# A chunked linear recurrence: inverting 32x32 triangular blocks on VectorE, or 16x16 blocks there and the rest as small products on TensorE

## The chip, the cores and the metric

The kernel runs on one core of a Trainium2 chip. The metric is the device time of one execution in microseconds; the time of a kernel is the median of its runs, and smaller is better.

## The reference

A recurrence over 768 steps for 4 batches of 8 heads, with a 40x40 state each, and behind it a mixture of eight experts over the 3072 tokens that it makes. All of it is float32.

```python
for t in range(S):                       # S = 768, B = 4, H = 8, D = 40
    y[:, :, t] = einsum('bhd,bhde->bhe', r[t], state)
    Sa = einsum('bhde,bhe->bhd', state, a[t])
    state = state * w[t][:, :, None, :] - einsum('bhd,bhe->bhde', Sa, b[t])
    state = state + einsum('bhd,bhe->bhde', v[t], k[t])
...
x = y.transpose(0, 2, 1, 3).reshape(B * S, H * D)      # 3072 x 320
P = np.exp(x @ w_gate - max)
for _ in range(8):                       # rows, then columns, normalised
    P /= P.sum(1, keepdims=True) + 1e-09
    P /= P.sum(0, keepdims=True) + 1e-09
    P *= N / E
for e in range(E):                       # E = 8, F = 1024
    out += P[:, e:e + 1] * (np.maximum(x @ w1[e], 0.0) @ w2[e])
```

## The kernel before

**Two parts.** The recurrence comes first (the function `attention`), and then the experts (`body`). The expert part is two large products per expert (L571 and L636), each made of three products of high and low parts, with ScalarE and VectorE between them. The change does not touch it. Its weights (L499) and its tokens (`xs`, L534 and L536, read back from the DRAM tensor `xd` into which the recurrence writes y) are loaded on SyncE's queue, SP, and the first of these loads stand among the recurrence's last ones.

**Chunks.** The recurrence is cut into 12 chunks of 64 steps. Within a chunk the state update is a system of 64 equations with a unit triangular matrix I - L for each batch and head, so a chunk needs T, the 64x64 inverse, for 4 x 8 = 32 pairs of batch and head. Two heads lie side by side on the 128 partitions, so a batch has 4 pairs of heads (NP = 4), and a T tile `tt` holds, for each of 16 pairs, a 128x128 matrix that is block diagonal: two heads, each with two 32x32 blocks on its diagonal and one 32x32 block beside them.

**The step of one batch in one chunk** (`recur`, 48 in all) is a chain: `av` (L280, products with the state) is masked by VectorE into `f`; `xc` (L288) makes the right-hand sides, which ScalarE copies to `x1` and `c1` (L294, L295); `pu` (L299) multiplies by T; VectorE masks it to `pm` (L301); `c2` (L306), `ws` on VectorE (L308), `y` and `z` on GpSimd, `zt` (L326, a transpose), and two copies by ScalarE into `rv` (L329, the state for this batch's next chunk). `lp` (L336) is the gate's product for the experts. The four batches run staggered.

**Preparations** (`prep`, one for each chunk and batch, ahead of the steps) load `inp`, make two scans on VectorE (`q`, `g`), scaled copies `kb` and `ab` (GpSimd, the first ones partly VectorE), the products `ll` (L158) and the transposes `kt` (L166), and from these by ScalarE and VectorE the operands `sx`, `bb`, and `lt` (L172), which goes to the DRAM tensor `ld`: that is L, for the inverse. From the seventh on ScalarE issues that store (L177).

**The inverse.** The chunks are taken two at a time (GROUPS). A group has 128 diagonal blocks of 32x32, and they are put on the 128 partitions, one each: `load_lu` loads them from `ld` into `lu`. VectorE inverts all of them at once: `inv_diag` column by column inside 8x8 blocks, `inv_8` joins these to 16x16 and `inv_16` (three calls with two contractions each) joins those to 32x32. A contraction (`contract`) is a broadcast multiplication and a reduction over its last axis (L192, L195). `un` is the inverse and `tn` its transpose, as far as each is needed, and `finish` stores both to DRAM (`ud`, `nd`; L362, L363).

**The rest of T.** For each chunk `tload` loads the diagonal 32x32 blocks into `tt` (L246, four loads) and what the block beside them needs into `lt` (L, L239 on; the transposed first block, L241) and `t2` (L242, the second block). `tmat` then makes that block by two products on 32x32 tiles of TensorE, 32 matmuls each: `gp` (L255), copied to `mt` by ScalarE (L257), and `op` (L261), copied into `tt` by ScalarE with four copies (L264). One such small matmul uses 32 rows and 32 columns of TensorE; up to four of them lie on different tiles of it.

**What sets the order.** `attention` writes the events (steps, loads, products, preparations, pieces of the inverse) into a list `ev` with a time each, five to a chunk, sorts it and issues them in that order; `tmat` does its work at a raised priority (T_PRI). The framework's scheduler then gives each engine a fixed order of instructions from that, which the engine keeps. Two `tt` buffers, 19 sets of preparation buffers and a pool of two PSUM buffers (`pt`: `gp`, `op`, `lp` and the first `kt`) bound what can run ahead. In the chunk loop SP's queue holds the loads of T and of the steps, and the stores of `un` and `tn`, in one order as well.

Of the kernel before, what the change touches and what calls it, by code (L numbers as in the profile page):

```python
# [11 lines left out]
F32 = mybir.dt.float32  # L12
# [17 lines left out]
def attention(ctx, tc, d, xd, ps, pq, pt, gs, lg):  # L30
    nc = tc.nc
# [10 lines left out]
    mask_f = cst[0:R2, 64:128]
    mask_p = cst[:, 128:232]
    ident = cst[:, 232:360]
    one65 = cst[0:RL, 400:660]

# [3 lines left out]
    for n in range(NCH * NB - NSX, NCH * NB):  # L50
        i, pool = n % NSX, sets[n - NCH * NB + NSX]
# [12 lines left out]
    tt_b = [const.tile([128, 4 * NP, 128], F32, name=f"tt{i}") for i in range(NTB)]  # L64
    ltt = const.tile([128, 2, 4 * NP, 32], F32, name="lt2")
    lt_b = [[ltt[i * 64:i * 64 + 64, k] for k in range(2)] for i in range(2)]
    t2_b = [const.tile([128, 2 * NP, 32], F32, name=f"t2{i}") for i in range(2)]
    mt = const.tile([128, 2 * NP, 32], F32, name="mt")
    ab_b = [pin.tile([R2, NP, 128], F32, name=f"ab{i}") for i in range(2)]
# [31 lines left out]
    def first_use(i):  # L101
        if i in fresh:
            fresh.discard(i)
            nc.gpsimd.memset(bb_b[i], 0.0)
            nc.scalar.copy(out=sx_b[i][64:R2].rearrange("r p h x -> r (p h) x")[:, :, 64:104],
                           in_=cst[64:R2, 360:400].unsqueeze(1).broadcast_to([40, 8, 40]))

    state = {"sx": 0, "ab": 0, "g1": 0, "rv": 0, "c1": 0, "lt": 0, "t2": 0, "tt": 0, "y": 0}

    def rot(key, lst):  # L110
        i = state[key]
        state[key] = (i + 1) % len(lst)
        return lst[i]
# [133 lines left out]

    def tmat(c):
        tt, (lb, t1, t2) = tts[c], tls[c]
        hq = [slice(q * 32, q * 32 + 32) for q in range(4)]  # L250
        with tc.high_priority(T_PRI):
            gp = pt.tile([128, 2 * NP, 32], F32, name="gp", tag="pt")
            for g in range(4 * NP):
                for h in range(2):
                    nc.tensor.matmul(gp[hq[g % 2 * 2 + h], g // 2], lhsT=lb[hq[h], g], rhs=t1[hq[h], g],  # L255
                                     start=True, stop=True)
            nc.scalar.copy(out=mt, in_=gp)  # L257
            op = pt.tile([128, 2 * NP, 32], F32, name="op", tag="pt")
            for g in range(2 * NP):
                for q in range(4):  # L260
                    nc.tensor.matmul(op[hq[q], g], lhsT=mt[hq[q], g], rhs=t2[hq[q], g], start=True, stop=True)  # L261
            for q in range(4):
                r = q % 2 * 64
                nc.scalar.copy(out=tt[r:r + 32, q // 2::2, r + 32:r + 64], in_=op[hq[q]])  # L264

# [93 lines left out]
    def finish(s, us):  # L359
        nc.vector.tensor_copy(out=tn[us, 16:32, 0:16], in_=un[us, 0:16, 16:32].rearrange("u c j -> u j c"))  # L360
        for o in range(0, us.stop, 64):
            nc.sync.dma_start(out=invs[s][1][o:o + 64], in_=un[o:o + 64])  # L362
# [29 lines left out]
    for s, cs in enumerate(GROUPS):  # L392
        us = slice(0, 64 * len(cs))
        t0 = 5 * cs[0] - 10
        n = len(cs) * NB
        for i in range(n):
            cb = (cs[0] + i // NB, i % NB)
            j = cb[0] * NB + cb[1] - NSX
            t = 5 * (j // 4) + 3 + SKEW * (j % 4) + 0.01
            t = max(t, t0 + P0[s] + PD * i) if s else -20 + 0.01 * i  # L400
            ev.append((t, do_prep, (s,) + cb + (i == 0,)))
        t += 0.02
        ev.append((t, load_lu, (s, len(cs))))
# [14 lines left out]
INV_DT = 0.05  # L418
# [35 lines left out]
def body(ctx, tc, d, out):  # L454
# [303 lines left out]
def _layout(inputs):  # L758
# [40 lines left out]
    cst[64:128, 64:128] = 1.0
    cst[0:64, 128:192] = up  # L800
    cst[64:128, 128:192] = up
    cst[:, 192:232] = 1.0
    cst[:, 232:360] = np.eye(128)
    cst[64:104, 360:400] = np.eye(40)
    cst[:, 400::65] = 1.0
    arrays = dict(inp=inp, rv=np.concatenate([rb, packed(g["v"])], -1), vt=vt, wts=wts, gate=gate, cst=cst)
# [18 lines left out]
```

## Time and profile before

| | |
|---|---|
| median of 3 runs | 1821.08 us (1817.26 to 1829.43) |
| the profiled execution | 1816.42 us, span 1814.0 us |
| mean granted clock of TensorE | 0.954 |
| busy in the span: TensorE matmuls | 1686.0 us, 93% |
| VectorE | 1366.1 us, 75% |
| ScalarE | 842.8 us, 46% |
| GpSimd | 876.6 us, 48% |
| DMA | 135.61 MB in 178736 packets, 119189 of them under 512 bytes |
| chain that ended last | 72% TensorE: L636 37%, L571 34% |
| first expert product (L571) | at 477.6 us |

The granted clock is the share of its full speed at which TensorE was allowed to run. Busy shares are means over two parts with different limits, and the profile has to be read by stretches. In the profile's rows an arrow points from what is read to what is written (`pu<-x,tt`), a number behind an x counts instructions, and what stands behind a second arrow is what ended the idle time before them. Numbers of buffers are left out there (`lt2` is `lt`, `t20` is `t`, `x1` is `x`).

### The profile page before, as it was taken

What the parts mean: (1) busy time and instruction counts of PE and PEld (TensorE: products, weight loads), DVE (VectorE), ACT (ScalarE), POOL (GpSimd) and SP (SyncE); (2) the same over time, 40 slices, a digit from 0 to 9 for tenths busy, and PEclk for the clock granted to TensorE, in tenths of its full rate; (3) what the DMA queues carried; (4) which work ended last, traced back from release to release, by engine and by line L of the source; (5) the groups of instructions that cost most, each with busy time, mean ns of one, the idle gap of its engine ahead of it and who ended that gap; (6) DMA issues with size and microseconds to landing.
All of it is one profiled execution on the core that took longest, in us unless ns stands there. A gap on an engine that the chain in (4) does not pass through costs nothing.

```text
span 1814.0 us, 32745 instructions
## 1 busy us (share of the span) xinstructions
PE 1686.0 (93%) x12611; PEld 1662.1 (92%) x12611; DVE 1366.1 (75%) x2353; ACT 842.8 (46%) x1811; POOL 876.6 (48%) x850
## 2 busy tenths in 40 slices
PE   5478888987889999999999999999999999999999
PEld 4367888887889999999999999999999999999999
DVE  7886976974788777767686778867686777768675
ACT  6357767765634443424343443435343443434342
POOL 7555645724453554728173554009173553719160
PEclk7569989998989999999999999999999999999999
DMA  7478678668221111102010112202010111102001
GB/s 200 106 160 197 150 173 192 153 142 200 75 67 36 41 38 38 58 20 76 8 69 20 57 38 72 58 1 76 14 63 22 55 38 38 58 20 76 18 21 44
DMA packets 178736, 135.61 MB, mean 75 GB/s; under 512 B 119189, under 2 KB 160789, under 8 KB 178581
## 3 DMA queue, kind: packets, MB, share of 16 engines
q1 hardware_dynamic: 174901, 127.79, 26.8%
q10 hardware_dynamic: 3680, 5.74, 1.2%
q8 instruction: 99, 1.62, 0.4%
q14 instruction: 56, 0.46, 0.1%
HBM read 111.48 MB, written 22.02 MB: 74 GB/s over the span
## 4 chain that ended last, share of the span: by engine, by line
PE 72%; DVE 6%; DMA 2%; issue 1%; SPq 1%; ACT 1%; POOL 1%; DVEq 0%; ACTq 0%; POOLq 0%
PE op L636 37%; PE p L571 34%; DVE pr L192 1%; DVE sm L589 1%; DVE hl L595 1%; DVE gt L195 0%; DMA ld<-lt 0%; PE xc L288 0%; DMA rv<-in_rv_dram 0%; DVE un L195 0%; PE pu L299 0%; DVE u L589 0%; DMA ws<-in_wts_dram 0%; DVE xch L559 0%; DMA lu<-ld 0%
## 5 line engine op out<-in xcount | busy, mean ns | idle before, releaser
L571 PE MATMUL p<-xch,wh 128*128 128x384 f32 (+1 forms) x1792 | 605.7, 339 | 10.2 <-DVE u L589 4.3
L592 ACT ACTIVATE hh<-sm 128x384 fp32r<-128x384 f32 x512 | 269.4, 527 | 723.0 <-DVE sm L589 722.9
L636 PE MATMUL op<-wh,hh 128*128 128x320 f32 x1536 | 477.1, 311 | 1.1 <-ACT hh L592 0.9
L636 PE MATMUL op<-wl,hh 128*128 128x320 f32 x1536 | 474.8, 310 | 0.0
L636 PE MATMUL op<-wh,hl 128*128 128x320 f32 x1536 | 468.2, 310 | 0.9 <-DVE hl L595 0.9
L517 POOL TENSOR_TENSOR wl<-ws,wh 128x640 fp32r<-128x640 f32 x60 | 103.6, 1726 | 606.3 <-ACT wh L515 606.1
L595 DVE SCALAR_TENSOR_TENSOR hl<-sm,hh 128x384 fp32r<-128x384 f32 x512 | 375.0, 766 | 1.8 <-ACT hh L592 1.3
L571 PEld LDWEIGHTS p<-xch,wh 128*128 128x128 f32 (+1 forms) x1792 | 337.2, 188 | 14.3 <-DVE u L589 6.0
L571 PE MATMUL p<-xcl,wh 128*128 128x384 f32 x896 | 302.6, 338 | 0.0
L571 PE MATMUL p<-xch,wl 128*128 128x384 f32 x896 | 301.7, 337 | 0.0
L636 PEld LDWEIGHTS op<-wh,hh 128*128 128x128 f32 x1536 | 290.3, 189 | 2.2 <-ACT hh L592 1.9
L636 PEld LDWEIGHTS op<-wl,hh 128*128 128x128 f32 x1536 | 291.1, 190 | 0.0
L636 PEld LDWEIGHTS op<-wh,hl 128*128 128x128 f32 x1536 | 287.3, 188 | 1.3 <-DVE hl L595 1.2
L589 DVE TENSOR_TENSOR sm<-p,u 128x384 f32<-128x384 f32 x384 | 236.1, 625 | 8.8
L571 PEld LDWEIGHTS p<-xcl,wh 128*128 128x128 f32 x896 | 168.7, 188 | 0.0
L571 PEld LDWEIGHTS p<-xch,wl 128*128 128x128 f32 x896 | 168.6, 188 | 0.0
L589 DVE TENSOR_TENSOR sm<-p,p 128x384 f32<-128x384 f32 x128 | 71.3, 557 | 128.7 <-PE p L571 74.7
L589 DVE TENSOR_TENSOR p<-p,p 128x384 f32<-128x384 f32 x128 | 71.2, 556 | 99.6 <-PE p L571 99.1
L589 DVE TENSOR_TENSOR u<-p,p 128x384 f32<-128x384 f32 x128 | 70.8, 554 | 57.6 <-PE p L571 56.4
L158 PE MATMUL ll<-ab,kb 104*128 104x128 f32 x336 | 62.4, 343 | 51.8 <-POOL ab L153 32.3
L158 PEld LDWEIGHTS ll<-ab,kb 104*128 104x128 f32 x336 | 53.4, 241 | 58.3 <-POOL ab L153 35.8
L525 POOL TENSOR_TENSOR wl<-ss,wh 128x512 fp32r<-128x512 f32 x60 | 90.1, 1502 | 27.6 <-ACT wh L522 23.4
(164 smaller groups left out, 2637.0 us busy)
## 6 DMA issues: line engine op xcount, KB each, us to landing
ws<-in_wts_dram SPq DMA_DIRECT2D x60, 832.0 KB, 4.4
inp<-in_inp_dram SPq DMA_DIRECT2D x42, 451.5 KB, 4.8
rv<-in_rv_dram SPq DMA_DIRECT2D x48, 336.0 KB, 4.1
xd<-y SPq DMA_DIRECT2D x24, 224.0 KB, 3.1
ld<-lt ACTq DMA_DIRECT2D x40, 128.0 KB, 2.9
f<-in_vt_dram SPq DMA_DIRECT2D x48, 80.0 KB, 3.1
out_dram<-acc SPq DMA_DIRECT2D x42, 80.0 KB, 2.1
lu<-ld SPq DMA_DIRECT2D x24, 128.0 KB, 3.2
```

Source lines behind the costliest of these rows:

```text
L158: nc.tensor.matmul(ll[:, p], lhsT=kb[:, p], rhs=ab[:, p], start=True, stop=True)
L192: nc.vector.tensor_tensor(out=prv, in0=a.unsqueeze(2).broadcast_to([nu, n_c, n_r, n_k]), in1=m.unsqueeze(1).broadcast_to([nu, n_c, n_r, n_ ...
L517: g.tensor_tensor(out=wl[:, 0:640], in0=raw[:, 256:896], in1=wh[:, 0:640], op=ALU.subtract)
L525: g.tensor_tensor(out=lv[:, 3:7], in0=so[:, :, 0], in1=hv[:, 3:7, 0], op=ALU.subtract)
L571: nc.tensor.matmul(o, lhsT=w_, rhs=x_, start=(j == 0), stop=(j == 3))
L589: eng.tensor_tensor(out=out, in0=x, in1=y, op=ALU.add)
L592: nc.scalar.activation(out=hh[:, f, h], in_=sm[f][:, h], func=AF.Relu)
L595: v.scalar_tensor_tensor(out=hl[:, f, h], in0=sm[f][:, h], scalar=0.0, in1=hh[:, f, h], op0=ALU.max, op1=ALU.subtract)
L636: nc.tensor.matmul(ops[i], lhsT=a[:, h, cs], rhs=w_[:, cw], start=(f == 0 and h == 0 and j == 0), stop=(last and h == 1 and j == 2))
```

## The change

`N_FINE = 6` covers all six groups, so that every group takes the new way:

- **VectorE** stops at 16x16: the three `inv_16` no longer run. In their place `flip_8` has GpSimd copy the 16x16 block of L beside the two inverted ones into the free corner of `un`, and `side` copies the second inverted block into the free corner of `tn` (`finish` made a copy of that size before). `flip_8` also has the first copy of the former `flip_l`; the second one (L200) goes.
- **TensorE** makes the 32x32 inverses out of these: `ga` and `wb`, 64 products of 16x16 each on four tiles, give the corner of each 32x32 block and put it into `tt`. `tp` transposes the first 32x32 block of each head, by 32 products with the identity. `gp` and `op`, 32 products each, make the block beside the diagonal as before, but lie on two tiles each.
- **ScalarE** copies each result out of PSUM by tile: four copies behind `ga`, four behind `wb`, two each behind `tp`, `gp` and `op`, in place of one and four.
- **Loads of T** are 7 a chunk, not 8: two of L (`lm`), one of `nd` for all 64 blocks (`vt`), four of the diagonal blocks (`tt`), the last in this order. `load_lu` puts the two blocks of a head on neighbouring partitions.
- The constants lose 64 columns: two masks share their storage. The function `flat` and the old way stay in the code, for groups from N_FINE on, and do not run.

In the new numbering `ga`, `wb`, `gp` and `op` are all L267, `tp` is L283, `ll` L156, `kt` L164, `pu` L329, `xc` L318, `av` L310, `c2` L336, `zt` L356 and `lp` L366; the loads are L249 (`lm`), L251 (`vt`), L254 (`tt`), and the copies L275, L279, L286, L290 and L294.

```diff
+    def flip_8(us):
+        lh = half_t(luf, us)
+        nc.vector.tensor_copy(out=lh[:, :, 8:16, 0:8], in_=lh[:, :, 0:8, 8:16].rearrange("u b k r -> u b r k"))
+        nc.gpsimd.tensor_copy(out=un[us, 0:16, 16:32], in_=lu[us, 0:16, 16:32])
+    def side(us):
+        nc.vector.tensor_copy(out=tn[us, 0:16, 16:32], in_=un[us, 16:32, 16:32])
-    INV = [(flip_l, ())] + [(inv_diag, (i,)) for i in range(1, 8)] + [(flip_d, ())]
-    INV += [(inv_8, (0,)), (inv_8, (1,)), (flip_h, ()), (inv_16, (0,)), (inv_16, (1,)), (inv_16, (2,))]
+    INV8 = [(inv_diag, (i,)) for i in range(1, 8)] + [(flip_d, ()), (inv_8, (0,)), (inv_8, (1,)), (flip_h, ())]
+    INV16 = [(flip_8, ())] + INV8 + [(side, ())]
...
     def tload(c):
...
-        u = [slice(cc * 64 + blk * 32, cc * 64 + blk * 32 + 32) for blk in range(2)]
-        for h in range(2):
-            nc.sync.dma_start(out=lb[h * 32:h * 32 + 32],
+        u = slice(cc * 64, cc * 64 + 64)
+        for h in range(0, 2):
+            nc.sync.dma_start(out=lm[h * 64:h * 64 + 32],
                               in_=ld[cc, 0:32].rearrange("j b p h s -> j (b p) h s")[:, :, h, 32:64])
-        nc.sync.dma_start(out=t1, in_=nd[u[0]].rearrange("(g h) j s -> (h j) g s", h=2))
-        nc.sync.dma_start(out=t2, in_=ud[u[1]].rearrange("(g q) j s -> (q j) g s", q=4))
-        for h in range(2):
-            for blk in range(2):
-                r = slice(h * 64 + blk * 32, h * 64 + blk * 32 + 32)
-                nc.sync.dma_start(out=tt[r, :, r], in_=ud[u[blk]].rearrange("(g h) j s -> (h j) g s", h=2)[h * 32:h * 32 + 32])
+        nc.sync.dma_start(out=vt, in_=nd[u].rearrange("(g q) j s -> (q j) g s", q=4))
+        for q in range(4):
+            r = slice(q * 32, q * 32 + 32)
+            nc.sync.dma_start(out=tt[r, :, r], in_=ud[u].rearrange("(g q) j s -> q j g s", q=4)[q])
...
+        hq = [slice(q * 32, q * 32 + 32) for q in range(4)]
+        xq = [slice(q * 32, q * 32 + 16) for q in range(4)]
+        yq = [slice(q * 32 + 16, q * 32 + 32) for q in range(4)]
+        lo, hi = slice(0, 16), slice(16, 32)
+        def products(name, tiles, lhs, rhs, n):
+            o = pt.tile([128, 4 * NP, n], F32, name=name, tag="pt")
+            for g in range(4 * NP):
+                for r, q in tiles:
+                    nc.tensor.matmul(o[r, g], lhsT=lhs(q, g), rhs=rhs(q, g), start=True, stop=True)
+            return o
         with tc.high_priority(T_PRI):
...
+                ga = products("ga", [(xq[q], q) for q in range(4)],
+                              lambda q, g: tt[xq[q], g, yq[q]], lambda q, g: vt[xq[q], g, lo], 16)
                 for q in range(4):
+                    nc.scalar.copy(out=vt[xq[q], :, lo], in_=ga[xq[q]])
+                wb = products("wb", [(xq[q], q) for q in range(4)],
+                              lambda q, g: vt[xq[q], g, lo], lambda q, g: vt[xq[q], g, hi], 16)
+                for q in range(4):
+                    nc.scalar.copy(out=tt[xq[q], :, yq[q]], in_=wb[xq[q]])
+                tp = pt.tile([128, 4 * NP, 32], F32, name="tp", tag="pt")
+                for g in range(4 * NP):
+                    for q in (0, 2):
+                        nc.tensor.matmul(tp[hq[q], g], lhsT=tt[hq[q], g, hq[q]], rhs=ident[hq[q], hq[q]],
+                                         start=True, stop=True)
+                for q in (0, 2):
+                    nc.scalar.copy(out=vt[hq[q]], in_=tp[hq[q]])
+            gp = products("gp", [(hq[q + 1], q) for q in (0, 2)],
+                          lambda q, g: lm[hq[q], g], lambda q, g: vt[hq[q], g], 32)
+            for q in (1, 3):
+                nc.scalar.copy(out=lm[hq[q]], in_=gp[hq[q]])
+            op = products("op", [(hq[q - 1], q) for q in (1, 3)],
+                          lambda q, g: lm[hq[q], g], lambda q, g: tt[hq[q], g, hq[q]], 32)
+            for q in (0, 2):
+                nc.scalar.copy(out=tt[hq[q], :, hq[q + 1]], in_=op[hq[q]])
...
-                u0, r0 = cc * 64 + blk * 32, blk * 32
-                nc.sync.dma_start(out=lu[u0:u0 + 32],
+                r0 = blk * 32
+                nc.sync.dma_start(out=lu[cc * 64 + blk:cc * 64 + 64:2],
...
+N_FINE = 6
```

**Where the products stand.** TensorE's order at the start, with the preparations (`ll`, `kt`) and the first T. Before, the first `gp` stands behind the 17th `ll`, and `op` and the first `pu` behind the 18th:

```order
L158 MATMUL ll_972<-ab0_204,kb_962 128x128 x4
L166 MATMUL kt_977<-cst_144,kb_962 128x104 x4
L255 MATMUL gp_850<-lt2_200 32x32 x32
L158 MATMUL ll_1029<-ab1_205,kb_1019 128x128 x4
L166 MATMUL kt_1034<-cst_144,kb_1019 128x104 x4
L261 MATMUL op_884<-t20_201,mt_203 32x32 x32
L255 MATMUL gp_1208<-lt2_200 32x32 x32
L299 MATMUL pu_946<-x1_931,tt0_198 128x104
```

Now, at the same place, from the first `ga`, which stands behind the 15th `ll`:

```order
L267 MATMUL ga_825<-vt0_202,tt0_198 16x16 x64
L156 MATMUL ll_757<-ab1_205,kb_747 128x128 x4
L164 MATMUL kt_762<-cst_144,kb_747 128x104 x4
L267 MATMUL wb_894<-vt0_202 16x16 x64
L156 MATMUL ll_1119<-ab0_204,kb_1109 128x128 x4
L164 MATMUL kt_1124<-cst_144,kb_1109 128x104 x4
L283 MATMUL tp_963<-cst_144,tt0_198 32x32 x32
L156 MATMUL ll_1176<-ab1_205,kb_1166 128x128 x4
L164 MATMUL kt_1181<-cst_144,kb_1166 128x104 x4
L267 MATMUL gp_998<-vt0_202,lm0_200 32x32 x32
L156 MATMUL ll_1250<-ab0_204,kb_1240 128x128 x4
L164 MATMUL kt_1255<-cst_144,kb_1240 128x104 x4
```

`op` is the next row, behind the 19th `ll`; between two of T's five products there is one preparation.

TensorE's order in the chunk loop, at chunk 2's T. Before, its two products stand within one step of a batch, and the second one breaks a product `xc` in two:

```order
L306 MATMUL c2_1779<-pm_1659,bb6_186 104x104 x3
L255 MATMUL gp_1701<-lt2_200 32x32 x32
L158 MATMUL ll_1638<-ab0_204,kb_1630 128x128 x4
L166 MATMUL kt_1643<-cst_144,kb_1630 128x104 x4
L306 MATMUL c2_1779<-pm_1659,bb6_186 104x104
L299 MATMUL pu_1819<-x1_1677,tt1_199 128x104 x4
L288 MATMUL xc0_1826<-f_1691,sx8_193 104x104
L261 MATMUL op_1735<-t20_201,mt_203 32x32 x32
```

Now, from `ga` to just behind `wb`:

```order
L267 MATMUL ga_2006<-vt0_202,tt0_198 16x16 x64
L156 MATMUL ll_1739<-ab0_204,kb_1731 128x128 x4
L164 MATMUL kt_1744<-cst_144,kb_1731 128x104 x4
L356 MATMUL zt_1794<-cst_144,z_1723 40x104 x4
L336 MATMUL c2_1801<-pm_1760,bb4_178 104x104 x4
L329 MATMUL pu_1849<-x1_1778,tt1_199 128x104 x4
L267 MATMUL wb_2075<-vt0_202 16x16 x64
L318 MATMUL xc0_1862<-f_1784,sx6_185 104x104 x4
```

`tp`, `gp` and `op` follow at distances like this, so the five products spread over about three steps of a batch. The last use of this buffer `tt0` for an earlier chunk stands about two steps ahead of `ga`, and the first `pu` with the new T one step behind `op`.

SP's queue where the last T is loaded and the expert part's first loads (`ws`, `xs`) begin. Before:

```order
L241 DMA lt2_200<-nd_3375 64x16x32
L242 DMA t21_202<-ud_3374 128x8x32
L269 DMA rv4_211<-in_rv_dram 112x4x192
L269 DMA rv0_207<-in_rv_dram 112x4x192
L499 DMA ws_5552<-in_wts_dram 128x1664
L246 DMA tt1_199<-ud_3374 32x16x32 x4
L499 DMA ws_5568<-in_wts_dram 128x1664
```

Now:

```order
L569 DMA xs_7564<-xd_57 128x2x256
L571 DMA xs_7564<-xd_57 32x2x256 x4
L345 DMA xd_57<-y0_214 448x1x128
L569 DMA xs_7582<-xd_57 128x2x256
L571 DMA xs_7582<-xd_57 32x2x256 x3
L301 DMA f_6395<-in_vt_dram 64x8x40
L571 DMA xs_7582<-xd_57 32x2x256
L249 DMA lm1_201<-ld_4339 32x16x32
L299 DMA rv1_208<-in_rv_dram 112x4x192
L249 DMA lm1_201<-ld_4339 32x16x32
L251 DMA vt1_203<-nd_4341 128x16x32
L254 DMA tt0_198<-ud_4340 32x16x32 x4
```

The first two `ws` and these two `xs` now stand ahead of the last diagonal blocks' loads; before, the first `ws` stood ahead of the last one, and the first `xs` behind it.

More of the change, by code (lines that the diff above doesn't have):

```diff
@@ L37, in attention @@
     dr = ctx.enter_context(tc.tile_pool(name="a_dr", bufs=2, space=bass.MemoryType.DRAM))
-    cst = const.tile([128, 64 + 64 + 104 + 128 + 40 + 260], F32, name="cst")
+    cst = const.tile([128, 64 + 104 + 128 + 40 + 260], F32, name="cst")
     nc.sync.dma_start(out=cst, in_=d["cst"])
     mask_u = cst[0:64, 0:64]
[L42 to L45, printed above, removed]
+    mask_f = cst[0:R2, 0:64]
+    mask_p = cst[:, 64:168]
+    ident = cst[:, 168:296]
+    one65 = cst[0:RL, 336:596]
     NTB = 2
@@ L64, in attention @@
     tt_b = [const.tile([128, 4 * NP, 128], F32, name=f"tt{i}") for i in range(NTB)]
[L65 to L68, printed above, removed]
+    lm_b = [const.tile([128, 4 * NP, 32], F32, name=f"lm{i}") for i in range(2)]
+    vt_b = [const.tile([128, 4 * NP, 32], F32, name=f"vt{i}") for i in range(2)]
     ab_b = [pin.tile([R2, NP, 128], F32, name=f"ab{i}") for i in range(2)]
@@ L105, in first_use @@
             nc.scalar.copy(out=sx_b[i][64:R2].rearrange("r p h x -> r (p h) x")[:, :, 64:104],
-                           in_=cst[64:R2, 360:400].unsqueeze(1).broadcast_to([40, 8, 40]))
-    state = {"sx": 0, "ab": 0, "g1": 0, "rv": 0, "c1": 0, "lt": 0, "t2": 0, "tt": 0, "y": 0}
+                           in_=cst[64:R2, 296:336].unsqueeze(1).broadcast_to([40, 8, 40]))
+    state = {"sx": 0, "ab": 0, "g1": 0, "rv": 0, "c1": 0, "lm": 0, "vt": 0, "tt": 0, "y": 0}
     def rot(key, lst):
@@ L232, in tload, with flat @@
+    def side(us):
+        nc.vector.tensor_copy(out=tn[us, 0:16, 16:32], in_=un[us, 16:32, 16:32])
+    def flat(us):
+        nc.gpsimd.memset(tn[us, 0:16, 16:32], 0.0)
+    INV8 = [(inv_diag, (i,)) for i in range(1, 8)] + [(flip_d, ()), (inv_8, (0,)), (inv_8, (1,)), (flip_h, ())]
+    INV16 = [(flip_8, ())] + INV8 + [(side, ())]
+    INV = [(flip_l, ())] + INV8 + [(inv_16, (0,)), (inv_16, (1,)), (inv_16, (2,))]
     def tload(c):
-        tt, (lb, t1), t2 = rot("tt", tt_b), rot("lt", lt_b), rot("t2", t2_b)
@@ L248, in tmat @@
+        for q in range(4):
+            r = slice(q * 32, q * 32 + 32)
+            nc.sync.dma_start(out=tt[r, :, r], in_=ud[u].rearrange("(g q) j s -> q j g s", q=4)[q])
     def tmat(c):
-        tt, (lb, t1, t2) = tts[c], tls[c]
+        tt, (lm, vt) = tts[c], tls[c]
         hq = [slice(q * 32, q * 32 + 32) for q in range(4)]
-        with tc.high_priority(T_PRI):
[L252 to L259, printed above, removed]
-                for q in range(4):
[L261 to L264, printed above, removed]
+        xq = [slice(q * 32, q * 32 + 16) for q in range(4)]
@@ L359, in finish @@
     def finish(s, us):
-        nc.vector.tensor_copy(out=tn[us, 16:32, 0:16], in_=un[us, 0:16, 16:32].rearrange("u c j -> u j c"))
+        if s >= N_FINE:
+            nc.vector.tensor_copy(out=tn[us, 16:32, 0:16], in_=un[us, 0:16, 16:32].rearrange("u c j -> u j c"))
         for o in range(0, us.stop, 64):
@@ L403, in attention @@
         ev.append((t, load_lu, (s, len(cs))))
-        for i, (fn, a) in enumerate(INV):
-            ev.append((t + INV_DT * 10 * i / len(INV), fn, (us,) + a))
+        if s == N_FINE:
+            ev.append((t, flat, (us,)))
+        ops = INV16 if s < N_FINE else INV
+        for i, (fn, a) in enumerate(ops):
+            ev.append((t + INV_DT * 10 * i / len(ops), fn, (us,) + a))
         ev.append((t + INV_DT * 10 + 0.01, finish, (s, us)))
@@ L478, in body @@
     nc.gpsimd.memset(ones, 1.0)
-    nc.sync.dma_start(out=ident, in_=d["cst"][:, 232:360])
+    nc.sync.dma_start(out=ident, in_=d["cst"][:, 168:296])
     po = ctx.enter_context(tc.tile_pool(name="po", bufs=1, space=bass.MemoryType.PSUM))
@@ L793, in _layout @@
     gate[0:40], gate[64:104] = wg[0], wg[1]
-    cst = np.zeros((128, 660), np.float32)
+    cst = np.zeros((128, 596), np.float32)
     i = np.arange(64)
@@ L797, in _layout @@
     cst[0:64, 0:64] = up
+    cst[64:128, 0:64] = 1.0
     cst[0:64, 64:128] = up
[L799 to L805, printed above, removed]
+    cst[64:128, 64:128] = up
+    cst[:, 128:168] = 1.0
+    cst[:, 168:296] = np.eye(128)
+    cst[64:104, 296:336] = np.eye(40)
+    cst[:, 336::65] = 1.0
     arrays = dict(inp=inp, rv=np.concatenate([rb, packed(g["v"])], -1), vt=vt, wts=wts, gate=gate, cst=cst)
```

4 lines of the change are left out of this document (3 added, 1 removed).

## The prediction

> **What bounds the kernel now.** I read the slices of the page first, to see where the recurrence ends.
>
> ```profile
> PE   5478888987889999999999999999999999999999
> PEclk7569989998989999999999999999999999999999
> DMA  7478678668221111102010112202010111102001
> ```
>
> A slice is 45 us. From the twelfth on TensorE is full at full clock: that is the expert part, which the change does not touch. So the time can only move in the first 485 us: at the start (TensorE half idle), along the chunks (eight to nine tenths, clock dipping), and where the two parts meet. Next the stretches between the products with T (L299, four a chunk, one per batch), by the view of stages and by the timeline:
>
> ```profile
> 121.96 1.06 PE L299 MATMUL pu<-x,tt 128*128 128x104 f32 x8
> ...
> 163.56 1.06 PE L299 MATMUL pu<-x,tt 128*128 128x104 f32 x8
> ...
> 188.66 1.14 PE L299 MATMUL pu<-x,tt 128*128 128x104 f32 x8
> ...
> 386.37 1.06 PE L299 MATMUL pu<-x,tt 128*128 128x104 f32 x8
> ```
> ```profile
> core 0: us, PE busy (x) PEld busy (x) DVE busy (x) ACT busy (x) POOL busy (x), PEclk, DMA share, GB/s
> 122.00:164.00 42.00, 37.96 (x422) 36.71 (x421) 35.15 (x54) 34.62 (x86) 30.56 (x35) 1.00 0.71 177
> 164.00:189.00 25.00, 18.57 (x315) 17.52 (x314) 15.87 (x38) 14.18 (x36) 10.41 (x15) 0.80 0.88 198
> 189.00:232.00 43.00, 38.30 (x350) 36.88 (x349) 40.73 (x64) 32.19 (x80) 31.53 (x35) 0.96 0.59 145
> 328.00:369.00 41.00, 37.43 (x401) 35.83 (x387) 37.40 (x59) 32.03 (x81) 29.49 (x30) 1.00 0.58 143
> ...
> 122.00:386.00 264.00, 226.30 (x2836) 217.12 (x2835) 209.77 (x378) 187.49 (x470) 154.03 (x179) 0.92 0.75 172
> 386.00:419.00 33.00, 30.97 (x417) 29.95 (x416) 27.14 (x41) 20.92 (x53) 7.84 (x10) 1.00 0.64 143
> ```
>
> The first and the last of these products are 32 batch steps apart: 264.4 us, 33.05 a chunk. Two kinds of stretch alternate. Inside a group of two chunks a step takes 41.6 / 6 = 6.9 us, with TensorE 90% busy, VectorE 84% (95% in 189 to 232) and ScalarE 82%. From one group to the next, two steps take 25.1 us instead of 13.9: no engine is above 75%, the DMA share is 0.88 and the clock 0.80. There T is late:
>
> ```profile
> 230.65 1.21 SPq L362 DMA_DIRECT2D ud<-un  x2
> 241.25 0.75 PE L255 MATMUL gp<-lt 32*32 32x32 f32 x64 [1.62 <-DMA lt<-nd]
> 244.47 1.50 ACT L264 COPY tt<-op 32x256 f32<-32x256 f32 x4 [1.15 <-PE op L261]
> 246.07 0.73 PE L299 MATMUL pu<-x,tt 128*128 128x104 f32 x2
> ```
>
> VectorE ends the inverse at 230.6, and 15.4 us of storing, loading, two products and copies later the next chunk uses T at once. So two things hold the chunks: three engines near full inside a group, and a late T between groups. Over the 264 us a chunk has 28.3 us of TensorE (226.3 / 8), 26.2 of VectorE, 23.4 of ScalarE.
>
> **The change part by part.** *VectorE.* Per group inv_16's six contractions over 1024 elements go:
>
> ```profile
> L192 DVE TENSOR_TENSOR pr<-gt,tn 128x1024 f32<-128x1024 f32 x18 | 21.9, 1218 | 0.0
> L192 DVE TENSOR_TENSOR pr<-un,lu 128x1024 f32<-128x1024 f32 x18 | 21.8, 1211 | 0.0
> L195 DVE TENSOR_REDUCE un<-pr 128x64 f32<-128x1024 f32 x12 | 14.4, 1203 | 0.0
> L195 DVE TENSOR_REDUCE gt<-pr 128x64 f32<-128x1024 f32 x12 | 14.4, 1200 | 0.0
> L195 DVE TENSOR_REDUCE un<-pr 128x128 f32<-128x1024 f32 x6 | 7.2, 1208 | 0.0
> L195 DVE TENSOR_REDUCE gt<-pr 128x128 f32<-128x1024 f32 x6 | 7.2, 1198 | 0.0
> L200 DVE COPY lu<-lu 128x256 f32<-128x256 f32 x6 | 2.2, 371 | 0.0
> ```
>
> That is 86.9 us, 14.5 a group; L200's copy becomes one of GpSimd's (2.2 us more; some 0.5 us each there, and GpSimd is busy 154 of 264). side() replaces finish's copy of the same size: nothing. So VectorE falls by 89.1 / 12 = 7.4 us a chunk, to 18.8, and T's blocks leave it 14.5 us earlier or more.
>
> *TensorE.* Two products of 32 matmuls become five: 64, 64, 32, 32, 32. Each matmul shows as two records.
>
> ```profile
> 164.46 0.35 PE L288 MATMUL xc<-f,sx 104*104 104x104 f32 x2
> 164.73 0.75 PE L261 MATMUL op<-t,mt 32*32 32x32 f32 x64
> 165.41 0.80 PE L288 MATMUL xc<-f,sx 104*104 104x104 f32 x6
> ```
>
> The third xc matmul would have started 0.18 us after 164.46; it starts at 165.41, and its first two run slower: a product of 64 records holds TensorE 0.86 us. Twice the records: 1.5. So a chunk has 2 x 1.5 + 3 x 0.86 = 5.6, plus about two more splits (the order breaks a product around another matmul; 0.2 each): 6.0 against 1.7, +4.3. The last three now use two tiles instead of four, which no row shows; if each tile sets its own pace they double: +6.5. The gp of before already alternates two row groups at full pace, so I take a value near the low end: +4.8. The Trainium skill (TensorE: Matmul & The Clock Gate, "Wait — 56ns, not 53.3ns?") has a rule that speaks against so many small matmuls: starts come no closer than about 25 ns however small they are. The row has 0.75 us for 64 records, 12 ns each, so on tiles the trace does not bear it out; by the rule a chunk's 448 records would take 11.2 us instead of 6.0.
>
> *ScalarE.* One copy of 256 elements and four of 256 become eight of 256 and six of 512:
>
> ```profile
> L264 ACT COPY tt<-op 32x256 f32<-32x256 f32 x48 | 17.5, 364 | 10.8 <-PE op L261 6.7 <-DMA inp<-in_inp_dram 3.0 <-ACT lt L172 0.5
> L257 ACT COPY mt<-gp 128x256 f32<-128x256 f32 x12 | 4.5, 373 | 7.0 <-PE gp L255 6.8
> L172 ACT ACTIVATE lt<-ll 64x512 f32<-64x512 f32 x42 | 24.9, 594 | 11.5 <-DVE sx L168 4.9 <-DVE st L168 4.5 <-DMA ld<-lt 1.2
> L177 ACTq DMA_DIRECT2D ld<-lt x40: 452/452/535, 50.4 to 368.1; - x40
> ```
>
> 8 x 0.364 + 6 x 0.594 = 6.5, less 1.8: +4.7 a chunk. ScalarE goes from 23.4 to 28.1, and with the four DMA issues of a chunk's preparations (0.45 each, not counted as busy) to 29.9.
>
> *DMA.* Seven loads a chunk for eight, the same 640 KB in the same 128-byte rows: one issue of 0.6 us saved on SP, nothing else. New is that the diagonal blocks must land before the first product, no longer only before the last copy. The order leaves about two batch steps (14 us) between the last use of that buffer and ga.
>
> ```profile
> issues: line engine op xcount, KB each, median us to landing
> tt<-ud SPq DMA_DIRECT2D x48, 64.0 KB, 3.1
> ```
>
> Four issues at the 0.6 each of L362's row and a landing of 3.1 are 5.5 us: covered, unless SP's queue stands still.
>
> *Start.* T's products stand between the preparations on TensorE: ga behind the 15th ll, then one preparation between stages, op behind the 19th.
>
> ```profile
> 45.63 2.08 PE L158 MATMUL ll<-ab,kb 104*128 104x128 f32 x8 [1.73 <-POOL kb L146]
> 50.47 2.04 PE L158 MATMUL ll<-ab,kb 104*128 104x128 f32 x8 [2.07 <-ACT lt L172]
> 70.18 2.08 PE L158 MATMUL ll<-ab,kb 104*128 104x128 f32 x8 [3.78 <-POOL kb L146]
> 96.94 2.08 PE L158 MATMUL ll<-ab,kb 104*128 104x128 f32 x8 [4.09 <-POOL ab L153]
> 112.97 0.76 PE L299 MATMUL pu<-x,tt 128*128 128x104 f32 x2
> ```
>
> Up to 70.18, the 13th, little changes. With VectorE inverting, the four preparations to 96.94 took 6.7 us each; without, 4.8 (45.63 to 50.47). Six more make the 19th start at 99 to 110, and op, its copies and the first pu follow 5 us later: 104 to 115 against 112.97. Of the 14.5 us saved some 5 arrive (+2 to -9), because five stages replace two.
>
> *Chunks.* Without the late T the clock should recover: 28.3 us of TensorE at 0.92 would be 26.0 at 1.00; I take half, 27.2, and add 4.8: 32.0. TensorE's fullest stretch is 386 to 419, 94%. 32.0 / 0.94 = 34.0 a chunk against 33.05: +1.0, over eight chunks +8. Ends: 30.4 / 0.94 = 32.3 (full clock, +4.4) gives -6; 34.0 / 0.91 = 37.4 (no clock gained, +5.7) gives +35. In 386 to 419 there is no late T to win back: 1.5 chunks x 4.8 / 0.94 = +7 (+4 to +9).
>
> *End.* From 419 TensorE has room for the last T. The expert part's first loads now stand ahead of the last two T loads on SP, which starts its preparation earlier and may delay T: -3 (-6 to +3).
>
> Sum: -5 + 8 + 7 - 3 = **+7 us**. The profiled execution took 1816.42 (span 1814.0), the runs' median is 1821.08, 4.7 above it; so 1823 for an execution like this one, 1828 beside the median.
>
> **The rivals.** *ScalarE becomes the bound* (slower). It needs 29.9 us a chunk in strict order, and every x1, f and rv copy of the recurrence stands behind T's fourteen. With issues it fills (32.19 + 2.25) / 43 = 80% of 189 to 232 and (32.03 + 2.25) / 41 = 84% of 328 to 369. If it gets no fuller than 82%, a chunk takes 36.5: +28 there, +27 in all, 1848. It decides from 84% down (35.5 a chunk, +19). Against it: in 122 to 164 it reached (34.62 + 2.7) / 42 = 89%, and then TensorE's 34.0 holds. *VectorE was the bound* (faster). For it speak its 95% in 189 to 232 and the late T; if with it gone TensorE runs without idle time at full clock, 30.4 a chunk, that is -21, and -24 with start, 386 to 419 (+5) and end: 1797. Against it: TensorE was never above 94%. *The floor per small matmul* (slower): 5.2 us more a chunk, over 9.5 chunks / 0.94 another +53, 1881. By the 25 ns rule, the trace disagreeing with 12.
>
> **How the numbers follow.** A measurement of this kernel tells about 1% from no change, here 18 us: 1803 to 1839. Forecast 0.49, ScalarE 0.30, floor 0.03, VectorE 0.18; so faster 0.18, same 0.49, slower 0.33. The likeliest is 1828. The range goes to 1803 below (the low ends of chunks, start and end, -18, and some of the VectorE case) and 1858 above (past the ScalarE case, toward the high end of +35 a stretch), leaving out about one in ten on each side.
>
> **What would show it.** Right: no group of L192 or L195 over 1024 elements; VectorE about 89 us less busy; first pu at 104 to 115; steps of 8 to 9 us all along, with no pause between groups; TensorE's clock near 1.0 from 122 on and its busy share above 90%; ScalarE near 88%. Wrong: long waits of ga for tt or vt (SP's queue), of wb, tp, gp or op for ScalarE's copies (the ScalarE case), products on two tiles near 1.6 us, or steps under 8 us with TensorE idle nowhere.

## The result, and the profile after

| | before | after |
|---|---|---|
| median | 1821.13 us | 1885.91 us (1877.96 to 1889.36) |
| ratio to before, 95% interval | | 1.0341 (1.0311 to 1.0371) |
| profiled execution, its span | 1816.42, 1814.0 us | 1883.93, 1882.1 us |
| VectorE busy | 1366.1 us | 1287.3 us |

The change costs 3.4%, 65 us; the forecast was 1828, with a range to 1858. The slices of the page, 47 us each now, show the same expert part behind a longer recurrence:

```profile
PE   5488989989798999999999999999999999999999
...
PEclk7568987987898999999999999999999999999999
```

TensorE is full from the fourteenth slice on; before it was from the thirteenth on. The last product with T starts at 553 us, before at 484 us. By stage, with the same columns as before, the middle row being the same 32 batch steps as 122.00:386.00 there (a product with T is eight records; the one at 133.24 stands in two pieces around `op`, and counts once):

```profile
core 0: us, PE busy (x) PEld busy (x) DVE busy (x) ACT busy (x) POOL busy (x), PEclk, DMA share, GB/s
116.90:553.50 436.60, 396.04 (x7410) 378.60 (x7411) 221.40 (x423) 299.71 (x713) 162.44 (x226) 0.86 0.60 138
127.20:433.20 306.00, 279.75 (x5275) 267.54 (x5271) 164.25 (x324) 221.02 (x535) 122.66 (x181) 0.87 0.65 146
433.20:553.50 120.30, 105.98 (x1910) 101.16 (x1909) 53.30 (x92) 73.81 (x167) 39.41 (x45) 0.86 0.46 117
```

The start is 5 us later (127.2 against 122.0), the 32 steps take 306.0 us instead of 264.4 (+42), and the rest to the last product with T 120.3 instead of 98.6 (+22), where the row before was:

```profile
386.40:485.00 98.60, 82.81 (x1015) 80.40 (x1014) 67.75 (x105) 60.40 (x139) 40.23 (x45) 0.91 0.60 144
```

VectorE is 54% busy in the 32 steps (79% before), ScalarE 72%, TensorE 91%, and its clock is 0.87, where it was 0.92. The groups of T's products and of their copies:

```profile
L283 PE MATMUL tp<-cst,tt 32*32 32x32 f32 x768 | 18.4, 205 | 1.7 <-issue 1.7
L267 PE MATMUL gp<-vt,lm 32*32 32x32 f32 x768 | 17.7, 199 | 0.0
L267 PE MATMUL wb<-vt 16*16 16x16 f32 x1536 | 17.5, 178 | 11.5 <-issue 11.5
L267 PE MATMUL op<-tt,lm 32*32 32x32 f32 x768 | 17.0, 196 | 0.2 <-ACT lm L290 0.2
L267 PE MATMUL ga<-vt,tt 16*16 16x16 f32 x1536 | 16.1, 179 | 0.2 <-DMA tt<-ud 0.2
```
```profile
L279 ACT COPY tt<-wb 16x256 f32<-16x256 f32 x48 | 17.4, 363 | 9.3 <-PE wb L267 8.2 <-ACT st L153 0.2
L275 ACT COPY vt<-ga 16x256 f32<-16x256 f32 x48 | 17.4, 363 | 3.5 <-PE ga L267 2.0 <-DMA tt<-ud 0.6
L290 ACT COPY lm<-gp 32x512 f32<-32x512 f32 x24 | 13.9, 578 | 3.7 <-PE gp L267 2.8 <-ACT bb L173 0.2
L286 ACT COPY vt<-tp 32x512 f32<-32x512 f32 x24 | 13.8, 576 | 6.8 <-PE tp L283 6.4
L294 ACT COPY tt<-op 32x512 f32<-32x512 f32 x24 | 13.8, 576 | 1.8 <-PE op L267 1.0 <-ACT lt L170 0.5
```

The late T is gone: nothing waits for T's loads any more but 0.2 us of `ga`. Before, `gp` waited 14.6 us for them:

```profile
L255 PE MATMUL gp<-lt 32*32 32x32 f32 x768 | 10.0, 205 | 14.6 <-DMA lt<-nd 14.6
```

In its place TensorE stops inside `wb`, for "issue", so for nothing that a semaphore ends, and the timeline shows one such stop (with a `ga` and a `gp` without one):

```profile
194.69 1.22 PE L267 MATMUL ga<-vt,tt 16*16 16x16 f32 x128
...
199.70 1.00 PE L267 MATMUL wb<-vt 16*16 16x16 f32 x103
203.11 0.34 PE L267 MATMUL wb<-vt 16*16 16x16 f32 x25 [2.41 <-issue]
...
213.25 1.20 PE L267 MATMUL gp<-vt,lm 32*32 32x32 f32 x64
```

103 of 128 records run, then 2.41 us of nothing, then the rest. The queue that carries instructions points to the reason (the second line is the kernel before):

```profile
q8 instruction: 129, 2.11, 0.5%
q8 instruction: 99, 1.62, 0.4%
```

129 packets are 16 KB each, and the trace has 33,199 records of TensorE (matmuls, weight loads and waits): 257 to a packet. Numbering those records, all eight stops inside `ga`, `wb` or `tp` with over 0.9 us from one matmul's start to the next (13.9 us in all) come behind a record whose number leaves 193 on division by 256, so always at the same place of a packet, and a fetch of 16 KB starts between 1.5 us ahead of the stop and 0.1 us behind its start (here at 200.6). Each stop ends 1.3 to 1.6 us behind the end of that fetch, so TensorE seems to have run through what it had fetched. Before, with 99 packets, it never stopped like that inside a product of T. The Trainium skill (Runtime: NRT & Kernel Launch, "Instruction fetch mechanics") has the same block, 16 KiB or 256 instructions, and calls the cost of crossing it mostly hidden; the trace agrees on the block, and not on the cost where 256 instructions run through in 1.2 us.

A second stop is VectorE's. Its queue reaches the first instruction of a group's inverse (L229) before the load it needs has come, and the recurrence behind it stands:

```profile
256.23 0.27 DVE L229 COPY lu<-lu 128x128 f32<-128x128 f32 x1 [6.03 <-DMA lu<-ld]
259.53 0.58 DVE L338 TENSOR_TENSOR ws<-c,c 104x416 f32<-104x416 f32 x1
...
260.17 2.03 PE L310 MATMUL av<-rv 104*104 104x128 f32 x8 [4.17 <-DVE ws L338]
```

### The profile page after: what moved, and what is told of

It reads as the page before. It is cut to its first block, busy times and chain, and to the rows that moved or that the text cites. A ratio compares the mean times of both kernels' runs of the same rounds, so it can differ in the third digit from the quotient of the medians.

```text
span 1882.1 us, 40444 instructions
## 1 busy us (share of the span) xinstructions
PE 1771.3 (94%) x16451; PEld 1741.6 (93%) x16451; DVE 1287.3 (68%) x2275; ACT 897.1 (48%) x1919; POOL 839.7 (45%) x856
## 4 chain that ended last, share of the span: by engine, by line
PE 83%; DVE 6%; DMA 4%; ACT 2%; issue 2%; POOL 1%; SPq 1%; ACTq 0%; DVEq 0%; POOLq 0%
PE op L671 35%; PE p L606 33%; PE xc L318 3%; PE pu L329 2%; PE av L310 2%; PE c L336 2%; DMA inp<-in_inp_dram 1%; PE ll L156 1%; DMA lu<-ld 1%; DMA ld<-lt 1%; PE zt L356 1%; PE lp L366 1%; DVE pr L181 1%; PE wb L267 1%; DVE q L124 1%
## 5 line engine op out<-in xcount | busy, mean ns | idle before, releaser
L560 POOL TENSOR_TENSOR wl<-ss,wh 128x512 fp32r<-128x512 f32 x60 | 89.9, 1498 | 28.3 <-ACT wh L557 24.1
L156 PE MATMUL ll<-ab,kb 104*128 104x128 f32 x336 | 67.4, 354 | 35.9 <-POOL kb L144 13.6
L156 PEld LDWEIGHTS ll<-ab,kb 104*128 104x128 f32 x336 | 56.6, 250 | 40.8 <-POOL kb L144 25.8
```

Source lines behind the costliest of these rows:

```text
L156: nc.tensor.matmul(ll[:, p], lhsT=kb[:, p], rhs=ab[:, p], start=True, stop=True)
L560: g.tensor_tensor(out=lv[:, 3:7], in0=so[:, :, 0], in1=hv[:, 3:7, 0], op=ALU.subtract)
```

## The experiments

Ratios are to the kernel before, run on the same chip. A us of difference between two kernels is their ratios' difference times 1821.

| kernel | ratio (95% interval) |
|---|---|
| no_fine | 1.0037 (1.0020 to 1.0053) |
| vector_alone | 0.9999 (0.9984 to 1.0014) |
| half_fine | 1.0179 (1.0150 to 1.0209) |
| tensor_alone | 1.0421 (1.0362 to 1.0480) |
| ga_twice | 1.0641 (1.0595 to 1.0687) |
| copies_vector | 1.0299 (1.0273 to 1.0325) |
| late_flip | 1.0267 (1.0242 to 1.0293) |
| spread | 1.0330 (1.0288 to 1.0371) |
| wide_twice | 1.0305 (1.0270 to 1.0340) |
| half_products | 1.0103 (1.0068 to 1.0139) |
| late_and_vector | 1.0320 (1.0291 to 1.0348) |
| spread_late_vector | 1.0295 (1.0263 to 1.0328) |
| burst_apart | 1.0488 (1.0439 to 1.0538) |
| one_burst | 1.0113 (1.0071 to 1.0155) |
| wide_all | 1.0415 (1.0376 to 1.0455) |
| before_wide | 1.0010 (0.9990 to 1.0030) |

**Which part costs.** `no_fine` and `half_fine`:

```diff
-N_FINE = 6
+N_FINE = 0      # half_fine: 3
```

> N_FINE = 0: VectorE inverts 32x32 blocks again and T needs two products, as before; the new load_lu, the seven loads in the new order and gp and op on two tiles stay. If the 65 us are the price of the 16x16 way itself (either theory, TensorE's work or its pauses), this is near the kernel before, 1821 to 1832 (gp and op take 1.2 us instead of 0.75 for 64 records, some 0.9 us a chunk more). If the loads' new order, or load_lu's stride, carries the loss, it is 1850 or more.

> N_FINE = 3: the first three groups (chunks 0 to 5) the new way, the last three the old way. If each chunk pays the same, about half of the loss: 1850 to 1858. If the loss sits in the last chunks, where the expert part's first loads and casts come in, it is under 1840; if it sits in the start and the first chunks, over 1870.

`vector_alone` and `tensor_alone`:

```diff
-            if GRP[c][0] < N_FINE:        # vector_alone
+            if GRP[c][0] < 0:
-    INV16 = [(flip_8, ())] + INV8 + [(side, ())]                # tensor_alone
+    INV16 = INV + [(corner, ()), (side, ())]    # corner: flip_8's copy on GpSimd
```

> VectorE still stops at 16x16, but ga, wb and tp with their copies are left out, so the corner of each 32x32 inverse is not computed. It shows what VectorE's 87 us are worth with TensorE's work as before. By the theory of work (TensorE bounds the chunks, VectorE's saving only removes the late T): 1800 to 1820, TensorE's clock at 0.93 or above. By the theory of pauses (VectorE, now nearly empty, runs ahead in its queue into waits for lu's load, and the recurrence behind it stops): 1825 to 1850, with TensorE idle before av for ws at the group's start as in the changed kernel (13 us in all).

> The five products on TensorE as in the changed kernel, but VectorE does its 32x32 inverse too (its result in the corner is overwritten by L again before it is stored), so that it is as busy as before. By the theory of work: T is late again and TensorE has the same work, 1890 to 1915. By the theory of pauses: the wait for lu is covered by VectorE's backlog, T is late instead; the fetch pauses stay, 1875 to 1895.

The new loads and the two-tile products, with their copies, cost 7 us together (`no_fine`), and half of the groups cost half. VectorE's saving is worth 7 us where T has two products (`vector_alone` against `no_fine`), and some 15 by the ratios, 6 by the medians, with intervals that overlap, where it has five (`tensor_alone` against the change). The 1892 us of `tensor_alone` lie in both of its expected ranges and do not tell them apart; `vector_alone` came out between its two. `ga`, `wb`, `tp` and their copies cost 62 (the change against `vector_alone`). Where VectorE's time went in `vector_alone` is a row of its waits, 99 to 491 us:

```profile
DVE q L124 <- DMA inp<-in_inp_dram: 54.9, 17, 5.2
```

and the same row in `no_fine`, 116 to 496 us:

```profile
DVE q L124 <- DMA inp<-in_inp_dram: 19.3, 6, 5.0
```

VectorE reaches the next preparation's scan sooner and waits there for its input. `vector_alone` has its first product with T at 99.1 us and its last at 490.9, `no_fine` at 115.8 and 496.4: of 17 us gained at the start 5 are left at the end.

**Work, or small instructions.** Six kernels give TensorE more to do. `ga_twice` and `wide_twice`, both on the changed kernel:

```diff
+                for g in range(4 * NP):                          # ga_twice
+                    for q in range(4):
+                        nc.tensor.matmul(ga[xq[q], g], lhsT=tt[xq[q], g, yq[q]], rhs=vt[xq[q], g, lo],
+                                         start=True, stop=True)
...
+            for _ in range(2 if b < 1 or b < 2 and p < 2 else 1):   # wide_twice
                 nc.tensor.matmul(pu[:, p], lhsT=tts[c][:, b * NP + p], rhs=x1[:, p], start=True, stop=True)
```

> ga's 64 products are issued twice into the same result: TensorE alone does more (1.22 us a chunk at full clock, 14.6 in all), nothing else changes. If the loop pays TensorE's work and no more, +15: 1900. If it pays work at the share of full-clock work that all kernels so far had in the loop (0.78: 290.9 of 372, 342.1 of 436.7), +19: 1904. If bursts of small instructions make TensorE wait for its own instructions (the pauses within wb that no semaphore ends, 2.4 us long, beside a fetch of 16 KB), 256 more of them a chunk lengthen these pauses: +25 to +45, 1910 to 1930.

> The changed kernel with six of a chunk's sixteen wide matmuls of pu (128x128, 104 columns) issued twice: 12 records of 0.112 us, 1.3 us of TensorE a chunk, as much as ga_twice added (1.22), but 24 instructions instead of 256 and over the whole array. If TensorE's time is what costs: +15 to +20 over the changed kernel, 1901 to 1906, and the clock as there. By the theory that the small instructions cost by their number (fetch) and by keeping the clock down, this is all that it costs, against +53 of ga_twice; if any 1.2 us added to a burst cost 53, 1939.

`wide_all` has `range(2)` there for every matmul; `before_wide` is `wide_twice` in the kernel before.

> The changed kernel with all sixteen wide matmuls of pu issued twice: 32 records of 0.112 us, 3.6 us of TensorE a chunk, 43 in all. By the theory that TensorE's time is the bound: +43 to +55, 1929 or more. By the theory that wide work fills the pauses and holds the clock up (wide_twice cost nothing): 1880 to 1900.

> The kernel before with wide_twice's six extra wide matmuls a chunk. If wide work pays for itself through the clock: 1810 to 1822. By TensorE's time: +15 to +20, 1836 to 1841.

`burst_apart` and `one_burst` put the 64 products of `ga_twice` elsewhere:

```diff
+    def burst(c):                 # an event at 5 * c + 2.4, queued behind the last matmul written
+        gd = pt.tile([128, 4 * NP, 16], F32, name="gd", tag="pt")
+        ...                       # 64 products like ga's, into gd
-            if GRP[c][0] < N_FINE:        # one_burst only
+            if GRP[c][0] < 0:
```

> The changed kernel with ga's 64 products done once more, into a result that nothing reads, but about one batch step ahead of ga instead of right behind it: the 256 instructions and 1.22 us of TensorE a chunk that ga_twice added, in a burst of their own. By the theory that a burst longer than what TensorE has fetched makes it wait for its instructions: +8 to +25 over the changed kernel, 1894 to 1911, against +53 of ga_twice. By the theory that it is the small tiles by their number, wherever they stand (they keep the clock down): +40 or more, 1926 to 1940.

> The same burst in vector_alone, where no ga, wb or tp stands: the price of one burst of 64 products a chunk with only gp and op beside it. If TensorE's idle time there takes it in: 1821 to 1828. If small tiles cost twice their time wherever they stand: 1845 or more. By its own time: +15, 1836.

`half_products` leaves half of the three new products out:

```diff
-        def products(name, tiles, lhs, rhs, n):
+        def products(name, tiles, lhs, rhs, n, ng=4 * NP):
...
-            for g in range(4 * NP):
+            for g in range(ng):           # 2 * NP for ga and wb; tp and the copies likewise
```

> ga, wb and tp and their copies for 8 of the 16 pairs only; the other corners are not computed. TensorE's work falls by 1.8 us a chunk (22 in all), its instructions by 320 a chunk. If the price goes with the work, half of the 65 between vector_alone (1821) and the changed kernel: 1850 to 1856. If the bursts cost more than in proportion (a burst shorter than what TensorE has fetched ahead waits for nothing): 1832 to 1846.

What each adds to the kernel that it is built on, beside the time that the added matmuls hold TensorE at full clock (`ga`'s row 1.22 us, `gp`'s 1.20, a wide record 0.112; twelve chunks):

| added | own time | measured | per us |
|---|---|---|---|
| wide, to before (before_wide) | 16 us | +2 | 0.1 |
| wide, to the change (wide_twice) | 16 | -7 | none |
| wide, to the change (wide_all) | 43 | +13 | 0.3 |
| half of ga, wb, tp and copies, to vector_alone (half_products) | 22 | +19 | 0.9 |
| the other half (the change) | 22 | +43 | 2.0 |
| one burst, to vector_alone (one_burst) | 15 | +21 | 1.4 |
| one burst apart, to the change (burst_apart) | 15 | +27 | 1.8 |
| the same burst behind ga (ga_twice) | 15 | +55 | 3.7 |

By the intervals of the ratios, a measured difference here is uncertain by 4 to 11 us: the -7 is no clear gain, and of the prices between 0.9 and 1.8 no two neighbours can be told apart. `ga_twice` came out above all that was expected of it, and `wide_twice` below.

TensorE's time by itself is not what is short: 43 us of wide matmuls cost 13. Small products cost about what they last or up to nearly four times that, and the same 64 cost twice as much behind `ga` as on their own. The wide ones stand in `pu`; none was put in the place of a burst, so what the place itself does to the price of a wide matmul is not shown. In `ga_twice` TensorE stops 15 times inside these products, for 38.7 us, 14 times at that place of a packet; in `burst_apart` 4 times, for 8.3 us. The 30 us between these sums agree with the 28 between the two ratios. One of the stops in `ga_twice`:

```profile
260.93 0.81 PE L276 MATMUL ga<-vt,tt 16*16 16x16 f32 x77
266.00 0.59 PE L276 MATMUL ga<-vt,tt 16*16 16x16 f32 x49 [4.26 <-issue]
```

**The clock.** From the first product with T to the last, `ga_twice`:

```profile
123.80:605.00 481.20, 420.69 (x8691) 405.36 (x8692) 221.60 (x421) 299.39 (x713) 164.79 (x226) 0.81 0.55 125
```

and `wide_all`:

```profile
117.80:567.80 450.00, 419.09 (x7796) 407.01 (x7797) 223.31 (x425) 300.09 (x713) 168.49 (x226) 0.91 0.59 134
```

The same time on TensorE, 420 us, once at clock 0.81 and once at 0.91. The trace grants the clock in windows of 3.41 us, at 1.0 or 0.5. Three pairs of windows of the changed kernel, and the time of `wb` in the first of them (L267 alone):

```profile
156.40:159.85 3.45, 2.79 (x144) 2.55 (x143) 0.71 (x2) 3.04 (x9) 1.35 (x3) 1.00 0.87 218
159.85:163.27 3.42, 3.42 (x21) 3.36 (x20) 1.97 (x4) 1.26 (x5) 0.86 (x2) 0.50 0.09 21
340.80:344.20 3.40, 2.70 (x27) 2.55 (x26) 3.37 (x10) 2.22 (x5) 1.64 (x3) 1.00 0.89 137
344.20:347.60 3.40, 3.19 (x28) 2.87 (x27) 3.37 (x9) 2.35 (x7) 1.52 (x2) 1.00 0.28 46
323.69:327.11 3.42, 3.42 (x70) 3.13 (x69) 0.00 (x0) 1.58 (x5) 0.00 (x0) 0.50 0.44 110
327.11:330.52 3.41, 3.41 (x20) 3.41 (x20) 1.16 (x2) 2.00 (x5) 1.18 (x1) 0.50 0.00 0
```
```profile
156.40:159.85 3.45, 1.36 (x128) 1.15 (x128) 1.00 0.87 218
```

Two windows are 80% busy; the one with 1.36 us of small products is followed by half clock, the one without by full. The third is busy throughout, mostly with `tp` (62 of its 70 records), and the half clock stays. Counted over the recurrences of all 18 kernels (2206 windows between the first and the last product with T; the columns are the share of a window in which small products of T, or those of an added burst, run):

```
                                     under 5%        25% or more
at full clock, 70 to 90% busy        4 of 95 fall    29 of 63 fall
at full clock, over 90% busy         0 of 473 fall   4 of 468 fall
at half clock, over 97% busy        56 of 269 stay   58 of 64 stay
```

So a burst of small tiles does not lower the clock of a window that is nearly full, but one with some idle time beside the burst falls far more often, and the half clock is seldom left. Of the six windows that left it, four are in `before` and `before_wide`, which have no 16x16 products. These are counts over traces; no run changed the clock alone. The Trainium skill (TensorE: Matmul & The Clock Gate, "Why this matters for your kernels") warns of idle gaps over about 3 us between bursts; here 0.66 us without work, the rest of the first window, went with the half clock beside small products.

**Other engines.** `copies_vector` has the fourteen copies as `nc.vector.tensor_copy`; `late_flip` puts L229 behind a later `ws`; `late_and_vector` has both:

```diff
+        t += INV_LATE if s else 0.0                   # INV_LATE = 3.0, for the inverse's pieces
...
+        with tc.issue_after(last[0]):                 # last[0]: the last ws written
             nc.vector.tensor_copy(out=lh[:, :, 8:16, 0:8], ...)
```

> The fourteen copies out of PSUM go to VectorE, which is busy half of the loop, instead of ScalarE. By the rival that ScalarE's strict order became the bound: 1850 to 1870. By the theories of TensorE's work and pauses: 1880 to 1892.

> The first instruction of each group's inverse on VectorE, which waits for lu's load, is put about one batch step later in VectorE's queue (from the third group on). If the pauses behind it (av for ws, 13 us, with the half clock behind each) cost what they last: 1865 to 1875. If the wait only moves (the inverse is later, T late), 1880 to 1892.

> late_flip and copies_vector together. If the two remove different waits, 10 + 15 come off: 1858 to 1864. If they remove the same one (the stop of the recurrence, which either makes good), 1866 to 1874.

`late_flip` takes 13 us off, the largest gain found; the copies on VectorE 8, with intervals that overlap; both together 4, less than either range that was expected. They do not add up: in the third VectorE holds copies at the head of its queue that wait for products (`zt` waits 13.4 us for `pm` in its trace, and TensorE stops 12.9 us inside `wb`).

`spread` cuts each product of T in two and puts the pieces between the recurrence's matmuls; `spread_late_vector` has all three:

```diff
+            for g0 in range(0, 4 * NP, PIECE):        # PIECE = 8
+                with tc.high_priority(T_PRI), tc.issue_after(anchor[0]):
+                    ...                               # the products of 8 pairs
+                yield                                 # next piece 0.3 later, next product 0.45 more
-T_LEAD = 2
+T_LEAD = 5
```

> Each of T's five products is cut in two pieces that stand apart between the recurrence's matmuls, and T is begun three units earlier. TensorE enters the small tiles more often: seven more splits a chunk at 0.2 us are +17 of work. By the theory of fetch: the pauses within wb (issue, 12 us of idle time) go, and with them seven dips of the clock, some 15 us: 1870 to 1885. By the theory of work: the pauses may go but 1895 to 1910.

> spread, late_flip and copies_vector together. If the pauses for fetch, the wait for lu and ScalarE's copies are three separate prices: 1850 to 1860, with the clock still lower than before, since small tiles then stand in most of the clock's windows. If what is left is the small tiles' own work and the clock: 1862 to 1880.

The stops inside the products fall from 13.9 us to 3.8, and the first product with T comes at 97.2 us. But with its bursts cut TensorE is busy for 430 us of the recurrence at a clock of 0.84, against 396 at 0.86, and the total is the changed kernel's within the intervals. The pauses alone are thus not the price. No version of the 16x16 way came near the kernel before.

## Why the prediction was wrong

**The step that failed: "Without the late T the clock should recover".** The late T did go. But the chunk's 28.3 us of TensorE were put at 27.2 for a better clock, and the clock went from 0.92 to 0.87. The matmuls that are not T's, 1878 records in the 32 steps of either kernel, keep TensorE busy for 234.5 us of them instead of 216.5: 2.3 us a chunk more, where 1.1 less were forecast. All of TensorE's work is 279.75 / 8 = 35.0 us a chunk, not 32.0, and at the 91% that it fills a chunk takes 306.0 / 8 = 38.3 us. That step's high end, no clock gained, +5.7, 37.4 us a chunk and +35, is passed as well: +42.

The forecast took the half clock for a mark of the late T. `vector_alone` shows that this fails even without the new products. There `gp` waits for no load, and from the second chunk on T is complete 11 to 33 us ahead of its first use (before, four of the twelve were complete only 0.1 to 1.5 us ahead). Yet the clock in the same 32 steps is 0.92, as it was before, and they take 271.8 us:

```profile
L267 PE MATMUL gp<-vt,lm 32*32 32x32 f32 x768 | 16.6, 203 | 0.0
```
```profile
111.80:383.60 271.80, 233.98 (x2851) 226.87 (x2852) 167.93 (x334) 192.75 (x467) 129.29 (x184) 0.92 0.79 169
```

TensorE's largest wait in these steps was not for T before either: it was 16.5 us for `ab` from GpSimd, and 6.2 us of `gp` for its load. The first of these stays in `vector_alone`, with 13.6 us. The change then adds small products, with which the clock is lower still, and stops of their own.

**TensorE's work: right in size, at the high end.** T's groups are 86.7 us, 7.2 a chunk against 1.7, so +5.6, for +4.8 forecast between 4.3 and 6.5. On two tiles 64 records take 1.20 us, not 0.75: nearer the doubling, which was given as the high end and not taken.

**The price of it: wrong.** Dividing by a fill of 94% treats all of TensorE's time alike. The runs show 0 to 0.3 us for a us of wide matmuls, 0.9 to 1.8 for short bursts of small ones, 2.0 for the second half of `ga`, `wb` and `tp`, 3.7 for a lengthened burst.

**VectorE: right, and the rival rejected rightly.** Its busy time fell by 78.8 us of the 89 forecast, and that is worth 7. The waits that took its place (L229 for `lu`, the scan for its input) were not foreseen.

**The start: wrong sign.** +4 for the first product with T (116.9), forecast at 104 to 115. `vector_alone` had it at 99.1: the three products between the preparations cost 18 us there, for "some 5 arrive".

**The end:** forecast +7 and -3 behind 386, measured +22. From there on stand 14 steps, three and a half chunks; the sum had charged one and a half and given the rest room. There was none: TensorE's busy time grows by 23.2 us (82.8 to 106.0), 6.6 a chunk, as in the 32 steps before them (53.1 us for eight chunks), and its idle time hardly moves (15.8 to 14.3). Two single waits of 4.6 and 3.3 us there are for ScalarE's `c` and VectorE's `f`, behind the expert part's work on these engines (491 to 503 us). SP's order did not show as a wait.

**ScalarE as the bound: not so.** It had +4.5 us a chunk (76.3 us of copies, 22.0 before), as forecast, but was 72% busy, and without the copies the kernel gained 8, with intervals that overlap.

**The floor per small matmul: its time of 1881 came close by luck, by another mechanism.** 128 records of `ga` take 1.22 us, 9.5 ns each; no floor shows.

**A reading of the page:** the prediction has TensorE full from the twelfth slice on; the digits say the thirteenth. Nothing in the sum hangs on it.

**Open:** what holds the clock of `vector_alone` at 0.92; how much of the price of one short burst is the clock and how much the recurrence's chain behind it; how the 7 us of `no_fine` divide between the loads and the two tiles, which was not tried.

## What to carry to other kernels

Before work moves to TensorE as many tiny matmuls, count its instructions and look at how they cluster: here a burst that ran through its fetched instructions stopped, and beside idle time the clock fell more often with small tiles in the window, while wide matmuls cost next to nothing. An engine that is relieved in a fixed order does not give its time back; look at what stands next in its queue and when that can start. And where a stage's clock is low, find what kept it low in each window before counting on its recovery.

## What was not expected of the hardware

In the changed kernel TensorE stops for its own instructions, 0.96 to 2.6 us at a time, always at the same place of a 16 KB packet of 256 instructions. A window of 3.41 us that is busy throughout but a quarter or more in small tiles left the half clock in 6 of 64 cases, against 213 of 269 without them. And 16 us more of wide matmuls left the kernel before at 1.0010 (0.9990 to 1.0030).
